# Block-sparse attention with a channel mixer: near outputs and part of the second dense unit turned by VectorE and transfers instead of TensorE

## The chip, the core and the metric

The program runs on one core of a Trainium2 chip. The metric is the device time of one execution in microseconds (us). The engines are PE (TensorE, with PEld for its weight loads), DVE (VectorE), ACT (ScalarE), POOL (GpSimd) and SP (SyncE, which here only issues DMA transfers). Each engine runs its instructions strictly in program order and waits on semaphores for the others.

## What is computed

The reference is block-sparse attention of 4 batches, 8 heads, 768 tokens and 64 channels, in blocks of 32 tokens, and behind it a channel mixer on the 512 joined channels.

```python
mask = abs(blk_i - blk_j) <= 1           # neighbours
mask |= first and last block, as rows and as columns
mask[qb, sampled_blocks[qb]] = True      # 3 sampled blocks each
attn = softmax(where(mask, q @ k.T / 8, -1e9)); x = attn @ v   # (4, 768, 512)
xk = mu_k * x + (1 - mu_k) * x_prev      # x_prev: one token earlier
xr = mu_r * x + (1 - mu_r) * x_prev
out = sigmoid(xr @ w_r) * (relu(xk @ w_k) ** 2 @ w_v)
```

All of it is float32; the mixer's products are made as three products of rounded halves each.

## The kernel before

**Units.** Batches go in two pairs. For each pair there is first a dense unit (`wide_pair`): the 64 rows of the first and last block, against all 768 keys, in four steps hp of two heads (names `sw`, `pw`, `tw`, `ptw`, `o_-1`). Then come eleven near units m = 0 to 10 (`near_unit`): two blocks of each of two batches, 128 rows, against eight key blocks (names `s`, `p`, `tb`, `o`). In the order of all 24 units the first dense unit is number 0, the second number 12; the near units are 1 to 11 and 13 to 23.

**Steps of a unit.** PE makes scores, DVE scales, masks and takes the minimum (L439), ACT makes exponentials and their sums (L444), PE multiplies the probabilities by V (L565 for near, L603 for dense units). For that product the probabilities must lie with keys on partitions. For units up to 7 PE turns them (`turn`, L453) and ACT or DVE copies them out of PSUM. For near units from number 8 (`CARRY`) DVE turns 32x32 blocks (`carry`, L471) and four transfers, each from 32 partitions to 128, put the blocks in place. The dense units use PE: 12 transposes for each hp, in three groups of four.

**Outputs.** `finish` divides by the sums on DVE (`x`, L628), PE turns x in four transposes (`tx`, L622), and ACT copies the result into the mixer's input `xt` (L658). The kernel also holds a path (`apart`) that turns x on DVE and lays it by transfers; with OUT = 30 no unit takes it.

**Mixer.** Each of 6 tiles of 128 tokens for each pair has gates (`r`, L752), hidden layers (`h`, L772, L784) and products (`v`, L798). The last four tiles run as two double tiles (the hidden layer of both in one matmul). `split_x` makes the rounded halves of a tile's input from `xt` on DVE, ACT and POOL.

**Order.** Every step is numbered in the order of the program text; `ORDER` is a table of these numbers, written out, that sets the order on every engine. `PICK` is a table of letters that sets the engine of each copy, rounding and difference. SP's transfers stand in that order too: weights, Q, K (`KR`) and V (`VR`) for the units, probabilities (`p`), and outputs. V of a near unit fills all four `VR` buffers in turn, so V of the next unit loads only when PE has used them. Buffers named `pt` (4 of them) hold x, turned probabilities and, in the double tiles, gates.

Of the kernel before, what the change touches and what calls it, by code (L numbers as in the profile page):

```python
# [159 lines left out]
def block_sparse_attention_channel_mix(ctx: ExitStack, tc: tile.TileContext, kt, kd, kw, qw, qn, vt, vn, vw, blocks, own_near, mu_k, mu_r, w_k, w_v, w_r, out):  # L160
# [187 lines left out]
    def load_wide(pr, i):  # L348
# [5 lines left out]
        def pair(hp):  # L354
            keys, values = ([], [])
            for i in range(PAIR):
# [8 lines left out]
                plan.add(SP, lambda r=r, hp=hp, i=i: nc.sync.dma_start(r.ap, kw[pr, hp, :, i]), writes=[(r.owner, *{k: 0 for one in r.keys for k in one})], size=wire(393216, 3072))  # L365
# [10 lines left out]
    def load_near(pr, m, i):  # L376
# [17 lines left out]
        for j in range(PAIR):  # L394
# [175 lines left out]
    def wide_pair(b, hp, q, t0, both, values, o, L):  # L570
# [15 lines left out]
        for row in range(2):  # L586
            keys = [(row, 0), (2 + row, W)]
            exp(ps_[row], slice(0, S), keys, nm, 2 + row, L, 2 * hp + row, t0 + W_EXP)
            parts += [(ps_[row], keys, lambda x, n=n: x[:, n * P:(n + 1) * P]) for n in range(6)]
            if b in CARRY_WIDE:  # L590
                carry(ps_[row], keys, f'w{b}_{hp}_{row}', 6)
        pts = [] if b in CARRY_WIDE else [turn(parts[4 * i:4 * i + 4], f'w{b}_{hp}_{i}') for i in range(3)]
        for row in range(2):
# [3 lines left out]
            def pv(h=h, mine=mine):  # L597
                for n, i in enumerate(mine):
                    for r in range(0 if pts else QB):
                        at = r * S // QB + n * BLK  # L600
                        nc.tensor.matmul(o.ap[ROWS[r], h * D:(h + 1) * D], ps_[h % 2].ap[:, at:at + BLK], values[r // PAIR].ap[:, n * P + h % 2 * D:n * P + (h % 2 + 1) * D], start=n == 0, stop=n == 5, skip_group_check=True)
                    for one, V in zip(HALF, values if pts else ()):
                        nc.tensor.matmul(o.ap[one, h * D:(h + 1) * D], pts[i // 4].ap[:, i % 4, one], V.ap[:, n * P + h % 2 * D:n * P + (h % 2 + 1) * D], start=n == 0, stop=n == 5, skip_group_check=True)  # L603
            plan.add(PE, pv, reads=([(pts[i // 4],) for i in mine[::2]] if pts else [(ps_[row], (row, 0), (2 + row, W))]) + [(V.owner, *V.keys) for V in values], writes=[(o, (hp, row))])

    def finish(b, m, i, o, parts, L):
# [19 lines left out]
        def divide():  # L626
            if apart or not DEAL:
                nc.vector.tensor_tensor(out=x.ap.rearrange('p (h d) -> p h d', d=D), in0=o.ap.rearrange('p (h d) -> p h d', d=D), in1=R.ap.unsqueeze(2).to_broadcast([P, H, D]), op=ALU.mult)  # L628
                return
            for half in range(2):  # L630
                nc.vector.tensor_tensor(out=x.ap.rearrange('p (c f k) -> p c k f', c=CC, k=QB)[:, :, 2 * half:2 * half + 2], in0=o.ap.rearrange('p (c k f) -> p c k f', c=CC, k=QB)[:, :, 2 * half:2 * half + 2], in1=R.ap.rearrange('p (c h) -> p h c', h=2)[:, half].unsqueeze(2).unsqueeze(3).to_broadcast([P, CC, 2, BLK]), op=ALU.mult)
# [440 lines left out]
```

## Time and profile before

| | |
|---|---|
| median of 3 runs | 528.49 us (528.47 to 529.82) |
| the profiled execution | 528.91 us, span 527.1 us |
| granted TensorE clock, mean | 0.997 |
| PE busy | 510.8 us, 97% |
| DVE / ACT / POOL busy | 355.7 / 313.2 / 213.5 us |
| DMA | 103.23 MB, 48164 packets, mean 196 GB/s |

The span is the time from the first to the last instruction; the execution is 1.8 us longer. The busy time of PE counts each matmul to its modelled end, so that a step in PE's stream is better read from the start of one group to the start of the next. The share of DMA is the mean busy share of the core's 16 DMA engines.

### The profile page before, as it was taken

The numbers are of one execution on the slowest core, as the hardware profiler recorded it, in microseconds if no ns is written. First come the engines' busy times: TensorE is split into PE (matmuls) and PEld (weight loads), VectorE is DVE, ScalarE is ACT, GpSimd is POOL, SyncE is SP. The second block draws the span as 40 slices with busy tenths as digits, with TensorE's granted clock in tenths as the row PEclk, the third lists the DMA queues.
The fourth block names the chain that finished last, engine by engine and source line by source line (L and its number), as shares of the span: only waits on it lengthen the run. The fifth ranks groups of instructions, "written<-read, shape, count | busy, mean of one in ns | idle before, by whom it ended". The sixth has DMA issues, their size and how long they took to land.

```text
span 527.1 us, 17633 instructions
## 1 busy us (share of the span) xinstructions
PE 510.8 (97%) x6935; PEld 407.3 (77%) x6935; DVE 355.7 (67%) x866; ACT 313.2 (59%) x785; POOL 213.5 (41%) x257
## 2 busy tenths in 40 slices
PE   7897999999999999999999999999999999999997
PEld 2464688779877887787987888888877788888886
DVE  4799899885887766566757676774898475441502
ACT  2789899876835574656565576467574365414430
POOL 0542545424611622552083174643261246605540
PEclk8999999999999999999999999999999999999999
DMA  8999794563678797468667787877866314010002
GB/s 289 405 321 353 277 351 146 174 222 101 183 244 240 231 319 239 170 224 248 209 191 237 244 259 215 234 238 203 238 198 184 113 31 141 0 67 15 1 0 80
DMA packets 48164, 103.23 MB, mean 196 GB/s; under 512 B 6929, under 2 KB 23442, under 8 KB 48082
## 3 DMA queue, kind: packets, MB, share of 16 engines
q1 hardware_dynamic: 47794, 101.72, 60.6%
q8 instruction: 54, 0.88, 0.7%
q10 hardware_dynamic: 288, 0.39, 0.2%
q14 instruction: 28, 0.23, 0.1%
HBM read 80.07 MB, written 6.29 MB: 164 GB/s over the span
## 4 chain that ended last, share of the span: by engine, by line
PE 77%; DMA 7%; SPq 5%; DVE 4%; ACT 4%; issue 2%; ACTq 0%; DVEq 0%
PE v L798 21%; PE o L565 7%; PE s L535 5%; PE r_0p L752 5%; PE r_1p L752 5%; PE h_3p L772 4%; PE h_2p L772 4%; PE h_1p L772 3%; PE h_0p L772 3%; DMA VR<-vn 2%; SPq L418 2%; DMA VR<-vt 2%; SPq L475 2%; PE sw L581 2%; DMA p<-tb 2%
## 5 line engine op out<-in xcount | busy, mean ns | idle before, releaser
L798 PE MATMUL v<-w,k 128*128 128x512 f32 (+1 forms) x600 | 141.5, 388 | 0.1
L798 PEld LDWEIGHTS v<-w,k 128*128 128x128 f32 x600 | 107.8, 188 | 25.0 <-issue 1.2
L439 DVE CUSTOM_DVE_ANT_1 p<-s,near_mask 128x256 f32<-128x256 f32 x152 | 84.0, 628 | 23.5 <-DMA p<-tb 12.9
L444 ACT ACTIVATE p<-p,nm 128x256 f32<-128x256 f32 x152 | 76.2, 503 | 33.1 <-DVE nm L439 30.9
L471 DVE STREAM_TRANSPOSE tb<-p 128x1024 f32<-128x1024 f32 x30 | 37.2, 1242 | 16.9 <-ACT p L444 11.3
L535 PE MATMUL s<-KR,q 64*32 64x256 f32 x1216 | 38.4, 380 | 0.0
L182 POOL COPY KR<-keys 128x256 f32 (+2 forms) x54 | 22.9, 462 | 27.8 <-DMA keys<-kw 13.7
L801 DVE SCALAR_TENSOR_TENSOR z<-v,z 128x512 f32<-128x512 f32 (+1 forms) x25 | 16.3, 660 | 25.8 <-PE v L798 25.8
L565 PEld LDWEIGHTS o<-VR,p 128*32 128x32 f32 x1920 | 27.9, 110 | 6.7 <-issue 4.0
L565 PE MATMUL o<-VR,p 128*32 128x64 f32 x1920 | 30.8, 220 | 1.6 <-DMA VR<-vn 0.8
L752 PE MATMUL r_1p<-w,xr 128*128 128x512 f32 x120 | 31.3, 404 | 0.0
L752 PE MATMUL r_0p<-w,xr 128*128 128x512 f32 x120 | 30.6, 401 | 0.2 <-DVE z L801 0.2
L535 PEld LDWEIGHTS s<-KR,q 64*32 64x32 f32 x1216 | 20.9, 106 | 10.7 <-issue 2.1
L731 POOL TENSOR_TENSOR xr<-xr_1f,xr 128x256 fp32r<-128x256 f32 x10 | 7.4, 739 | 53.0 <-ACT xr L180 39.9
L444 ACT ACTIVATION_READ_ACCUMULATOR p<-p,nm 128x1 f32 x152 | 28.8, 189 | 0.0
L752 PEld LDWEIGHTS r_0p<-w,xr 128*128 128x128 f32 x120 | 21.9, 188 | 6.5 <-PE sw L581 0.6
L762 POOL TENSOR_TENSOR h_0k<-h_0k 128x512 f32<-128x512 f32 x10 | 10.6, 1063 | 38.7 <-ACT k L761 38.7
L752 PEld LDWEIGHTS r_1p<-w,xr 128*128 128x128 f32 x120 | 21.6, 188 | 5.4 <-ACT h_3k L760 0.4
L772 PE MATMUL h_2p<-xk,w 128*128 128x256 f32 x192 | 25.1, 285 | 0.0
L772 PE MATMUL h_3p<-xk,w 128*128 128x256 f32 x192 | 25.1, 286 | 0.0
L772 PE MATMUL h_0p<-xk,w 128*128 128x256 f32 x192 | 25.0, 284 | 0.0
L772 PEld LDWEIGHTS h_1p<-xk,w 128*128 128x128 f32 x192 | 23.5, 189 | 1.6 <-ACT h_0k L760 0.8
(226 smaller groups left out, 1086.7 us busy)
## 6 DMA issues: line engine op xcount, KB each, us to landing
VR<-vn SPq DMA_DIRECT2D x42, 512.0 KB, 4.6
VR<-vt SPq DMA_DIRECT2D x130, 128.0 KB, 3.3
p<-tb SPq DMA_DIRECT2D x120, 128.0 KB, 3.2
KR<-kd SPq DMA_DIRECT2D x18, 512.0 KB, 4.6
out<-z SPq DMA_DIRECT2D x23, 256.0 KB, 2.7
q<-qn SPq DMA_DIRECT2D x22, 256.0 KB, 4.5
keys<-kw SPq DMA_DIRECT2D x14, 384.0 KB, 5.5
raw<-w_k SPq DMA_DIRECT2D x4, 1024.0 KB, 7.4
```

Of the source, the lines that this page charges most:

```text
L182: engine(on).tensor_copy(to, of)
L418: nc.sync.dma_start(to[:, i], vt[bass.ds(sampled_block(nc.sync, pr, m, j * NRAND + i) + pr * NB, 1)].rearrange('o k b x -> (o k) (b x)'))
L439: nc.vector.tensor_tensor_reduce(out=dealt(p.ap[:, cs]), in0=cut(view()), in1=by, scale=-SCALE, scalar=3e+38 if first is None else nm.ap[: ...
L444: plan.add(ACT, lambda: nc.scalar.activation(p.ap[:, cs], p.ap[:, cs], AF.Exp, bias=nm.ap[:, col:col + 1], scale=-1.0, accum_out=L.ap[:, h ...
L471: plan.add(DVE, lambda: nc.vector.transpose(out=turned.ap.rearrange('p (k y c) -> p k y c', k=QB, c=BLK), in_=p.ap.rearrange('p (y k c) -> ...
L535: nc.tensor.matmul(s.ap[ROWS[j], row, a * 256:(a + 1) * 256].rearrange('p (x g a) -> p g a x' if carried else 'p (x a g) -> p g a x', g=2, ...
L565: nc.tensor.matmul(o.ap[ROWS[j], h * D:(h + 1) * D], held[gi][1](i, g, j), VR[values[j % PAIR][g]].ap[:, j // PAIR, h * D:(h + 1) * D], st ...
L752: nc.tensor.matmul(pr.ap[:, 0:512], xr.ap[:, a, c, :], wr[c].ap[:, w, :], start=c == 0 and m == 0, stop=c == CC - 1 and m == 2)
L762: plan.add(POOL, lambda: nc.gpsimd.tensor_tensor(out=kk.ap, in0=kk.ap, in1=kk.ap, op=ALU.mult), reads=[(kk,)], writes=[(kk,)])
L772: nc.tensor.matmul(ph.ap[:, ff * PAIR * TT:(ff + 1) * PAIR * TT], wk[f // 4 * CC + c].ap[:, w, f % 4 * P:(f % 4 + 1) * P], xk.ap[:, a, c, ...
L798: nc.tensor.matmul(pv.ap[:, 0:width], hid[f][2](a), wv[f].ap[:, w, cs], start=f == 0 and m == 0, stop=f == FC - 1 and m == 2)
L801: plan.add(DVE, lambda pv=pv, cs=cs: nc.vector.scalar_tensor_tensor(out=z.ap[:, cs], in0=pv.ap[:, 0:width], scalar=unit, in1=z.ap[:, cs], ...
```

## The change

1. OUT goes from 30 to 9, so the outputs of near units from number 9 take the path `apart`: units 9 to 11 (m = 8 to 10 of the first pair) and 13 to 23 (all of the second), 14 by this count; the instructions show 14 too. x is turned by one DVE instruction whose read steps by four elements, and four transfers of 32x512 values lay it into `xt`, in pieces of 32 values (128 bytes).
2. The variant `DEAL`, off before, is removed.
3. CARRY_WIDE = (1,), AWAY = 4: in the second dense unit four of the six 128-key chunks of each head are turned by DVE and carried by four transfers of 64 KB (`carry_most`); the other two still by PE, one group of four for each hp instead of three. The product takes 32-row matmuls for the carried chunks and 64-row ones for the rest.
4. Keys of a dense unit come in one transfer of 768 KB for each hp instead of two of 384 KB (but for the first hp of the first unit).
5. SENT is empty, so its new branch does nothing.
6. ORDER and PICK are new: fewer ACT and more DVE copies of sampled keys among others.

```diff
-                plan.add(SP, lambda r=r, hp=hp, i=i: nc.sync.dma_start(r.ap, kw[pr, hp, :, i]), ...)
+                if i == PAIR - 1:
+                    plan.add(SP, lambda hp=hp: nc.sync.dma_start(whole[pr].ap[:, hp], kw[pr, hp]), ...)
...
+    def carry_most(p, keys, most, name):
+        size = QB * AWAY * BLK
+        turned = buf([P, size], F32, 'pt', PT_BUFS, f'tw{name}')
+        plan.add(DVE, lambda: nc.vector.transpose(out=turned.ap.rearrange('p (k y c) -> p k y c', k=QB, c=BLK), in_=p.ap[:, 0:size].rearrange('p (y k c) -> p k y c', k=QB, c=BLK)), reads=[(p, *keys)], writes=[(turned,)])
+
+        def away():
+            for r in (0, 2, 1, 3):
+                nc.sync.dma_start(p.ap[:, r * AWAY * BLK:(r + 1) * AWAY * BLK], turned.ap[r * BLK:(r + 1) * BLK])
+        plan.add(SP, away, reads=[(turned,)], writes=[(p, most)], ...)
...
-                carry(ps_[row], keys, f'w{b}_{hp}_{row}', 6)
-        pts = [] if b in CARRY_WIDE else [turn(parts[4 * i:4 * i + 4], f'w{b}_{hp}_{i}') for i in range(3)]
+                carry_most(ps_[row], keys, (row, 'most'), f'w{b}_{hp}_{row}')
+        away = AWAY if b in CARRY_WIDE else 0
+        rest = [x for i, x in enumerate(parts) if i % 6 >= away]
+        pts = [turn(rest[i:i + 4], f'w{b}_{hp}_{i // 4}') for i in range(0, len(rest), 4)]
...
-            plan.add(DVE, lambda: nc.vector.transpose(out=flip.ap.rearrange('p (k c f) -> p k c f', k=QB, f=BLK), in_=x.ap.rearrange('p (c k f) -> p k c f', k=QB, f=BLK)), ...)
+            plan.add(DVE, lambda: nc.vector.transpose(out=flip.ap.rearrange('p (k c f) -> p k c f', k=QB, f=BLK), in_=x.ap.rearrange('p (c f k) -> p k c f', k=QB, f=BLK)), ...)
...
-CARRY_WIDE = ()
-OUT = 30
-DEAL = OUT <= NP * NM
+SENT = ()
+CARRY_WIDE = (1,)
+AWAY = 4
+OUT = 9
...
-    "turn": "AAAADDAAAAADAAAAAADDAAAAAADDAAAAAADADDAAAAADDAADDDDA",
+    "turn": "AAAAAAAADAADDAAADAAAAADAAAAADDADDAAADDDDAADAA",
...
-    2, 13, 0, 119, 3, 15, 14, 24, 20, 22, 28, 27, 23, 45, 44, 21, 64, 65, 84, 25, 31, 85, 112, 16, 29, 114, 30, 33,
+    22, 3, 4, 14, 20, 0, 1, 116, 16, 24, 44, 28, 23, 2, 13, 30, 29, 21, 25, 31, 47, 33, 32, 50, 35, 34, 36, 37, 49,
```

On PE, in the second pair, behind the scores of its unit 2 and among the hidden layers of tile 4 (`h_4`), before and now:

```order
L535 MATMUL s_2_0_4770<-KR,q_2_4244 32x8x32 x16
L535 MATMUL s_2_1_4790<-KR,q_2_4244 32x8x32 x16
L622 MATMUL tx_0_4808<-ident,x_0_4757 128x128 x4
L772 MATMUL h_4_3p<-xk_4_4162,w_938 128x256 x6
L772 MATMUL h_4_3p<-xk_4_4162,w_1433 128x256 x6
```

```order
L789 MATMUL h_4_1p<-xk_4_4309,w_794 128x256 x6
L553 MATMUL s_2_1_4807<-KR,q_2_4557 32x8x32 x16
L553 MATMUL s_2_0_4830<-KR,q_2_4557 32x8x32 x16
L789 MATMUL h_4_2p<-xk_4_4309,w_901 128x256 x6
L789 MATMUL h_4_2p<-xk_4_4309,w_1404 128x256 x6
```

The four transposes of x of unit 0 (`tx_0`) are gone from the row; score and hidden matmuls follow each other.

On DVE, in the same pair, around the division of unit 0 (`x_0`), before and now:

```order
L439 ISA p_1_1_4502,nm_1_1_4503<-s_1_1_4445,near_mask 128x32x8
L439 ISA nm_1_1_4503 128x1
L471 STREAM_TRANSPOSE tb_1_1_4723<-p_1_1_4502 128x1024
L624 RECIPROCAL R_0_4615<-R_0_4615 128x8
L628 TENSOR_TENSOR x_0_4757<-o_0_4522,R_0_4615 128x512
L618 TENSOR_SCALAR R_1_4759<-L_1_4443 128x8
```

```order
L447 ISA nm_1_0_4686 128x1
L645 RECIPROCAL R_0_4472<-R_0_4472 128x8
L648 TENSOR_TENSOR x_0_4756<-o_0_4617,R_0_4472 128x512
L479 STREAM_TRANSPOSE tb_1_0_4765<-p_1_0_4685 128x1024
L652 STREAM_TRANSPOSE xf_0_4767<-x_0_4756 128x512
L743 SCALAR_TENSOR_TENSOR xr_4_1f_4798<-xr_4_1d_4785,mk,xt_4_3489 128x128
```

Behind the division now stands the turn of x into `xf_0`, one transpose of probabilities (`tb_1_0`) later.

On SP, in the second dense unit, where keys and V of that unit are loaded, before and now:

```order
L475 DMA p_10_0_3503<-tb_10_0_3704 128x1x256 x4
L365 DMA keys_3184<-kw 128x768 x2
L369 DMA VR_68<-vw 128x768
L369 DMA VR_71<-vw 128x768
L369 DMA VR_69<-vw 128x768
L369 DMA VR_70<-vw 128x768
L369 DMA VR_68<-vw 128x768
L369 DMA VR_69<-vw 128x768
L393 DMA KR<-kd 128x1024
L802 DMA out<-z_2_1_3443 128x512
L369 DMA VR_70<-vw 128x768
L369 DMA VR_71<-vw 128x768
```

```order
L493 DMA pw_0_1_3747<-tww_0_1_3769 128x1x128 x4
L370 DMA VR_68<-vw 128x768
L370 DMA VR_69<-vw 128x768
L493 DMA pw_0_0_3764<-tww_0_0_3794 128x1x128 x4
L370 DMA VR_71<-vw 128x768
L661 DMA xt_5_720<-xf_10_3897 128x4x32 x4
L370 DMA VR_70<-vw 128x768
L493 DMA pw_1_1_3871<-tww_1_1_3907 128x1x128 x4
L493 DMA pw_1_0_3951<-tww_1_0_4031 128x1x128 x4
L370 DMA VR_68<-vw 128x768
```

The carried probabilities (`pw` from `tww`) and the laid output of unit 10 (`xt` from `xf_10`) now stand between the loads of V; the keys have gone ahead of this place.

## Rows read from the trace of the kernel before

**Rows 1.** The page's part 1: busy us, share of the span, instructions.
```profile
PE 510.8 (97%) x6935; PEld 407.3 (77%) x6935; DVE 355.7 (67%) x866; ACT 313.2 (59%) x785; POOL 213.5 (41%) x257
```

**Rows 2.** Busy us (instructions) of PE, PEld, DVE, ACT, POOL by stretch; clock; DMA.
```profile
0.00:85.00 85.00, 74.71 (x1225) 47.77 (x1225) 70.95 (x153) 66.71 (x163) 34.76 (x49) 0.98 0.91 326
180.00:255.00 75.00, 74.93 (x1101) 59.97 (x1100) 49.01 (x142) 43.34 (x103) 26.72 (x38) 1.00 0.74 235
255.00:450.00 195.00, 193.43 (x2727) 161.20 (x2725) 134.32 (x328) 114.75 (x308) 90.23 (x109) 1.00 0.66 195
450.00:527.10 77.10, 73.70 (x341) 60.47 (x339) 24.38 (x49) 23.36 (x44) 28.08 (x30) 1.00 0.07 28
```

**Rows 3.** Timeline of PE: start, us, line, operation; first and last moved output.
```profile
182.80 0.66 PE L622 MATMUL tx<-ident,x 128*128 128x128 f32 x4
183.21 1.17 PE L798 MATMUL v<-w,k 128*128 128x512 f32 x4
...
449.13 0.60 PE L622 MATMUL tx<-ident,x 128*128 128x128 f32 x4
449.48 2.82 PE L798 MATMUL v<-w,k 128*128 128x512 f32 x11
```

**Rows 4.** Timeline of all engines behind the last near unit's product.
```profile
445.72 1.99 PE L565 MATMUL o<-VR,p 128*32 128x64 f32 x128
447.78 0.69 DVE L628 TENSOR_TENSOR x<-o,R 128x512 f32<-128x512 f32 x1 [5.49 <-PE o L565]
450.98 0.59 ACT L658 COPY xt<-tx 128x512 f32<-128x512 f32 x1
460.51 0.77 DVE L731 TENSOR_TENSOR later<-xk_5f,later 128x512 fp32r<-128x512 f32 x1
466.97 2.96 PE L784 MATMUL h_3p<-later,w 128*128 128x512 f32 x12
```

**Rows 5.** Groups by line on DVE: count, busy us, mean ns, idle before.
```profile
L471 DVE STREAM_TRANSPOSE tb<-p 128x1024 f32<-128x1024 f32 x30 | 37.2, 1242 | 16.9 <-ACT p L444 11.3 <-ACT KR L180 3.2 <-DMA p<-tb 1.6
L439 DVE CUSTOM_DVE_ANT_1 p<-s,near_mask 128x256 f32<-128x256 f32 x152 | 84.0, 628 | 23.5 <-DMA p<-tb 12.9 <-PE s L535 10.3
L439 DVE CUSTOM_DVE_ANT_1 pw<-sw,wide_mask,nmw 128x384 f32<-128x384 f32 x16 | 9.6, 617 | 3.8 <-PE sw L581 3.1
```

**Rows 6.** SP's issues and landing of carried probabilities: ns and us, min/median/max.
```profile
L475 SPq DMA_DIRECT2D p<-tb x120: 542/596/1661, 139.5 to 437.1; - x120
DMA to landing us min/median/max: 2.5/3.2/5.2
```

**Rows 7.** Timeline of PE, second dense unit: some of its turns and products.
```profile
218.36 0.60 PE L453 MATMUL tw<-ident,pw 128*128 128x128 f32 x4
218.88 1.62 PE L603 MATMUL o_-1_3970<-VR,ptw 128*64 128x64 f32 x48
220.44 1.09 PE L453 MATMUL tw<-ident,pw 128*128 128x128 f32 x8
221.46 1.52 PE L581 MATMUL sw<-keys,qw 64*64 64x384 f32 x16
...
236.65 0.60 PE L453 MATMUL tw<-ident,pw 128*128 128x128 f32 x4
237.00 3.73 PE L798 MATMUL v<-w,k 128*128 128x512 f32 x15
```

**Rows 8.** Timeline of PE: a near unit's product and what follows.
```profile
270.42 1.99 PE L565 MATMUL o<-VR,p 128*32 128x64 f32 x128
272.34 1.67 PE L752 MATMUL r_1p<-w,xr 128*128 128x512 f32 x6
```

**Rows 9.** Transfers in 430 to 438 us, carried probabilities almost alone: packets, DMA share.
```profile
DMA packets 884, 0.82 MB, mean 103 GB/s; under 512 B 94, under 2 KB 883, under 8 KB 883
q1 hardware_dynamic: 883, 0.81, 44.8%
```

**Rows 10.** The same in 469 to 478 us: four outputs alone, 2 KB pieces.
```profile
DMA packets 576, 1.05 MB, mean 117 GB/s; under 512 B 64, under 2 KB 64, under 8 KB 576
q1 hardware_dynamic: 576, 1.05, 30.4%
```

**Rows 11.** ACT's exponentials of the dense units: count, busy us, mean ns.
```profile
L444 ACT ACTIVATE pw<-pw,nmw 128x768 f32<-128x768 f32 x16 | 14.9, 933 | 9.9 <-DVE nmw L439 9.2 <-ACT xr L180 0.7
```

**Rows 12.** Timeline of PE at the start: second scores, waiting for keys.
```profile
8.59 1.56 PE L581 MATMUL sw<-keys,qw 64*64 64x384 f32 x8 [1.63 <-DMA keys<-kw]
```

**Rows 13.** What SP waited for in 255 to 450 us: total, times, longest.
```profile
SPq L411 <- PE o L565: 11.9, 5, 3.6
SPq L418 <- PE o L565: 9.8, 3, 4.1
```

More of the change, by code (lines that the diff above doesn't have):

```diff
@@ L364, in pair @@
                     continue
-                plan.add(SP, lambda r=r, hp=hp, i=i: nc.sync.dma_start(r.ap, kw[pr, hp, :, i]), writes=[(r.owner, *{k: 0 for one in r.keys for k in one})], size=wire(393216, 3072))
+                if i == PAIR - 1:
+                    plan.add(SP, lambda hp=hp: nc.sync.dma_start(whole[pr].ap[:, hp], kw[pr, hp]), writes=[(whole[pr], *[(hp, b, h) for b in range(PAIR) for h in range(2)])], size=wire(786432, 6144))
             for i in range(PAIR):
@@ L393, in load_near, with send @@
             plan.add(SP, lambda: nc.sync.dma_start(K.ap[:, WINDOW:WINDOW + 4].rearrange('p n a x -> p (n a x)'), kd[pr, :, n - 1:n + 3].rearrange('p n x -> p (n x)')), writes=[(K, 'near')], size=wire(524288, 4096))
-        for j in range(PAIR):
+        for j in range(PAIR if i in SENT else 0):
+            def send(j=j):
+                for r in range(NRAND):
+                    at = sampled_block(nc.sync, pr, m, j * NRAND + r) + pr * NB
+                    nc.sync.dma_start(K.ap[:, (NRAND + 1) * j + r].rearrange('p a x -> p (a x)'), kt[bass.ds(at, 1)].rearrange('o p x -> (o p) x'))
+            plan.add(SP, send, reads=[(packed,)], writes=[(K, ('far', j))], size=wire(131072, 1024) * NRAND, parts=NRAND)
+        for j in range(0 if i in SENT else PAIR):
             def fetch(j=j, key=PAIR * i + j):
@@ L476, in carry @@
         plan.add(SP, away, reads=[(turned,), (p, *keys)], writes=[(p, *keys)], size=QB * wire(22500 * wide, 128 * wide), parts=QB)
+    def carry_most(p, keys, most, name):
[5 more added lines that the diff above has]
+                nc.sync.dma_start(p.ap[:, r * AWAY * BLK:(r + 1) * AWAY * BLK], turned.ap[r * BLK:(r + 1) * BLK])
+        plan.add(SP, away, reads=[(turned,)], writes=[(p, most)], size=QB * wire(22500 * AWAY, 128 * AWAY), parts=QB)
     def first_scores(pr, m, gi, s, q, keys):
@@ L598, in pv @@
                 for n, i in enumerate(mine):
[L599 to L600 removed]
+                    i -= away * (i // 6 + 1)
+                    for r in range(QB if n < away else 0):
+                        at = (r * away + n) * BLK
                         nc.tensor.matmul(o.ap[ROWS[r], h * D:(h + 1) * D], ps_[h % 2].ap[:, at:at + BLK], values[r // PAIR].ap[:, n * P + h % 2 * D:n * P + (h % 2 + 1) * D], start=n == 0, stop=n == 5, skip_group_check=True)
[L602 removed]
+                    for one, V in zip(HALF, values if n >= away else ()):
                         nc.tensor.matmul(o.ap[one, h * D:(h + 1) * D], pts[i // 4].ap[:, i % 4, one], V.ap[:, n * P + h % 2 * D:n * P + (h % 2 + 1) * D], start=n == 0, stop=n == 5, skip_group_check=True)
[L604 removed]
+            plan.add(PE, pv, reads=([(pts[0],), (ps_[row], (row, 'most'))] if away else [(pts[i // 4],) for i in mine[::2]]) + [(V.owner, *V.keys) for V in values], writes=[(o, (hp, row))])
     def finish(b, m, i, o, parts, L):
@@ L626, in divide @@
         def divide():
[L627 to L631, printed above, removed]
+            nc.vector.tensor_tensor(out=x.ap.rearrange('p (h d) -> p h d', d=D), in0=o.ap.rearrange('p (h d) -> p h d', d=D), in1=R.ap.unsqueeze(2).to_broadcast([P, H, D]), op=ALU.mult)
         plan.add(DVE, divide, reads=[(o, *parts), (R,)], writes=[(x,)])
```

31 lines of the change are left out of this document (13 added, 18 removed), and 208 rows, old and new, of the table ORDER.

## The prediction

> **What bounds the kernel now.** First the busy shares of the page: PE is busy for 97% of the span, no other engine for more than 67% [rows 1]. Then the stretches: from 180 to 450 us PE is idle for 0.07 and 1.57 us (75.00 less 74.93, 195.00 less 193.43) and its clock is 1.00, the upper of its two levels [rows 2]. So here the end is set by how much PE has to do: work taken from its stream moves everything behind it, as long as what PE waits for still comes in time. The first 85 us are another matter: PE is idle for 10.3 us, DMA is busy at 0.91 and DVE for 71 of 85 us [rows 2]; there the loads set the pace. Behind 450 us transfers hardly matter (0.07). The second thing to read is what is close to being full in the stretches where the change puts its new work: DMA stands at 0.74 from 180 to 255 us (the second dense unit and units 8 to 10) and at 0.66 from 255 to 450 us (near units of the second pair) [rows 2]. DVE has 49 of 75 and 134 of 195 us there.
>
> **Outputs turned elsewhere.** A group of four `tx` costs PE the time from its start to the start of the next group: 0.41 us for the first moved unit, 0.35 us for the last [rows 3]; the 14 moved groups lie between 0.35 and 0.56 and sum to 5.6 us. All 14 stand in PE's full stretches, so I count 5.6 us as gain. No wait of PE is added in their place, since the consumer is the mixer tile, far behind: by the new order, with durations from the rows, 20.9 us of PE work lie between the last near unit's product and the first hidden layer of the last double tile. Before, that product starts at 445.72 and the last rounded half of the tile is ready at 461.28, 5.7 us before PE comes to it at 466.97 [rows 4]. The old way from divided x (448.47) to `xt` (451.57) takes 3.1 us [rows 4]; the new one is a turn, four issues and a landing: 0.62 us (half of 1242 ns, [rows 5]) to 0.95 us, 4 x 0.6 and 3.2 us [rows 6], or 6.2 to 6.6 us. The tile is later by 3.1 to 3.5 us, so at least 2.2 of the 5.7 us of margin stay. Cost on PE: 0.
>
> **The stepped read.** No row shows a DVE turn with a stepped read. Below stands half of the 1024-value turn, 0.62 us; above, the same times 1.5, the ratio per value of the near softmax pass with its stepped write (628 ns for 256) to the dense one (617 ns for 384) [rows 5], so 0.95 us. Fourteen of them are 9 to 13 us of DVE time, 8 turns of carried probabilities 5 us, and PICK moves 15 key copies to DVE. ACT loses the `xt` copies. DVE at 0.65 to 0.69 of the two stretches has room for it: 0 on the path.
>
> **Second dense unit.** PE's 12 groups of `tw` here cost 0.35 to 0.53 us each (0.52 for one, 1.02 for two together, 0.35 for the last, [rows 7]), 5.4 us in all or 0.45 each; 8 go: 3.6 us. The product of one hp took 1.56 us (218.88 to 220.44) for 48 matmuls of 64 rows, 32 ns each [rows 7]; a near product takes 1.92 us for 128 matmuls of 32 rows, 15 ns each [rows 8]. Now there are 256 of the small kind (3.8 us) and 64 of the large (2.1 us), 5.9 us instead of 6.2: a gain of 0.3 us. If the change of shape cost something at each switch it would be a few tenths; I leave it. PE's gain in sum: 5.6 + 3.6 + 0.3 = **9.5 us**.
>
> **What it gives back: transfers.** From 180 to 255 us DMA is busy for 0.74 x 75 = 55.5 us. To it come 32 transfers of carried probabilities (64 KB in pieces of 512 bytes) and 12 of laid outputs (64 KB in pieces of 128 bytes), while PE's stretch shrinks to 75 - 1.1 - 3.6 - 0.3 = 70 us. The nearest row is the carried near probabilities, also from 32 partitions to 128, in pieces of 1 KB: 0.448 x 8 us x 16 engines / 883 packets = 65 ns a piece, or 0.82 MB in 3.6 busy us = 229 GB/s [rows 9]. A 64 KB transfer then costs 0.29 us if bytes count; if pieces count, 0.52 us with 512 bytes and 2.08 us with 128 bytes. For the carried ones I take the middle, 0.40 us x 32 = 12.8 us. For the laid ones I take bytes, 0.29 x 12 = 3.4 us: outputs of 2 KB pieces run at 1.05 MB in 2.7 busy us, 384 GB/s [rows 10], with all 128 partitions as source, so the row's lower rate can come from its 32 source partitions, which the laid ones share, as well as from its pieces; both ends stay for the range. Sum 55.5 + 12.8 + 3.4 = 71.7 against 70: 1.7 us too much. On the Trainium skill's page "DMA: Bandwidth & Descriptors", section "Why small descriptors are slow (HBM only)", transfers within SBUF keep 78% of the link's rate with 128-byte packets; by that a laid transfer would be 0.37 us and the sum 1.0 us more. No row here shows such a piece.
>
> Besides, the new path from scores to product in that unit is long: four softmax passes of 0.62 us [rows 5], two exponentials of 0.93 us with their sums, 2.2 us [rows 11], a turn of 0.62, 8 issues of 0.6 us and a landing of 3.2 us [rows 6], 13.3 us. By the new order 12.9 us of PE work lie between scores and product of the last hp and 13.8 us for the first, where two loads of V also stand in SP's row (0.8 us). Late by 0.4 and 0.3 us on medians, and by 2 us more where a landing takes 5.2 us; I put 1.8 us. Given back in all: 3.5 us. In the stretch from 255 to 450 us the 44 laid transfers by bytes are 13 us on 129 of then 190 us: hidden.
>
> **The start.** Merged keys save issues but put 768 KB ahead of the second half of the first keys, for which PE waits now [rows 12]; at the 326 GB/s of that stretch [rows 2] that is 2.4 us later, and the next scores need no further wait. I take 0 and keep 2 us either way.
>
> **Sum.** 528.9 (the profiled execution) - 9.5 + 3.5 = 522.9; that execution lies 0.4 us above the median of the runs, so **522.5 us**.
>
> **Rivals.** (a) Transfers fit and PE never waits: the full 9.5 us, 519.0 us. For it: PE is full today with DMA at 0.74, and loads can be asked for earlier. Against: V of the dense unit can't load before PE has freed its buffers. (b) SP's row: each laid output is four issues, 2.4 us [rows 6], that wait for a turn on DVE and stand ahead of the next unit's V. Their cover is the time in which SP waits for PE to free those buffers anyway, 21.7 us in 255 to 450 us [rows 13]; 11 units need 26.4 us. The 4.7 us without cover go to PE through late V: 527.2 us, and 528 with a late turn or two. This counts as no change. (c) Slower: pieces of 128 bytes cost by the piece. The stretch of the second dense unit then fills with transfers that PE waits for. With 1.8 us for the chains it decides where 55.5 + 12.8 + 12 x = 70 + 7.7, x = 0.78 us, or 24 ns a piece. At 40 ns a laid transfer is 1.28 us, transfers are 83.7 us, and the time is 522.5 + (13.7 - 1.7) = 534.5 us. At 65 ns the second stretch overflows too (129 + 92 against 190 us) and it would be 574 us. For it: the 1 KB pieces run at 229 GB/s where 2 KB ones run at 384 [rows 9, 10]. Against: 65 ns is for eight times the bytes. The Trainium skill, same page, section "Specifications", speaks for (c): 512 bytes is the least piece at line rate, and below it the engine reads, changes and writes back. It gives no time, and no run here shows one.
>
> **How the numbers follow.** Forecast 0.42, (a) 0.20, (b) 0.15, (c) 0.23. A measurement of this kernel tells 0.3%, 1.6 us, from no change: faster means under 526.9 us. Faster 0.62, same 0.15, slower 0.23. The range reaches down to (a) with 2 us from the start and a little of today's waits, 516.5, and up to (c) at 40 ns, 534.5; what lies outside is about 2 in 10, most of it above.
>
> **What would show it.** PE's busy time down by some 9 to 13 us; 40 instead of 96 `tx` and no wait behind the last tile's hidden layers; DMA share from 180 to 255 us at 0.9 or more, with waits of PE for `pw` or `VR` of 2 to 4 us in that unit; laid transfers that land within 3 to 4 us. If DMA stays near 0.8 there, (a) holds; if laid transfers take over 0.8 us of all engines each, (c). Wrong altogether would be a PE wait at the tiles' first gates in the second pair, or a first 85 us that moved by over 2 us.

## The result, and the profile after

The changed kernel takes 536.4 us in the median (532.19 to 539.12) against 529.15 us (528.47 to 530.30) of the kernel before in the same session: **1.013 times** the time, interval 1.0097 to 1.0163. It is slower, above the range that was given (516.5 to 534.5). Its profiled execution is the longest of its four: 539.12 us, span 537.4 us, mean clock 0.990. That is 10.3 us of span more than the trace of before; the medians differ by 7.2 us.

The page's part 1 of the changed kernel, and the stretches of [rows 2] in its trace (busy us of PE, PEld, DVE, ACT, POOL; clock; DMA share; GB/s):

```profile
PE 508.1 (95%) x6971; PEld 402.5 (75%) x6975; DVE 361.4 (67%) x882; ACT 304.0 (57%) x761; POOL 222.3 (41%) x266
```

```profile
0.00:85.00 85.00, 71.43 (x1195) 46.87 (x1200) 68.36 (x148) 65.03 (x156) 39.60 (x48) 0.96 0.90 318
180.00:255.00 75.00, 68.38 (x1019) 51.41 (x1027) 50.22 (x130) 36.37 (x84) 26.94 (x37) 1.00 0.79 229
255.00:450.00 195.00, 190.50 (x2736) 157.28 (x2721) 138.18 (x353) 111.92 (x298) 82.10 (x104) 0.99 0.77 222
450.00:537.40 87.40, 83.45 (x503) 68.49 (x501) 31.30 (x66) 24.64 (x45) 32.56 (x34) 1.00 0.10 31
```

PE did lose work, but it now stands idle for 6.6 us from 180 to 255 us where it was full before, and for 4.5 us from 255 to 450. DMA isn't near full in either stretch (0.79 and 0.77). The longest waits of PE in the whole trace (us in total, times, longest) are all for transfers, yet small:

```profile
PE o L583 <- DMA VR<-vt: 2.5, 2, 2.1
PE sw L599 <- DMA keys<-kw: 2.4, 1, 2.4
PE o L583 <- DMA VR<-vn: 2.2, 1, 2.2
```

Waits alone don't show where the time went, because the new order also moves mixer work on PE from one place to another. So I counted PE's own work: the number of matmuls of each form that stand ahead of a given product in PE's row, times the duration of that form at full clock. It is an estimate, good to 1 or 2 us in a row of the table, and it takes no price for a change between forms. All of it is 502.1 us before and 494.0 us after, 8.1 us less. The time at which a product starts, less the work ahead of it, is how late PE is there:

| near unit's product (number in the order) | start, before / after | late, before / after / v_one_after (below) |
|---|---|---|
| 4 | 84.42 / 87.44 | 21.5 / 24.2 / 21.0 |
| 9 | 172.77 / 174.77 | 24.9 / 26.9 / 26.6 |
| 11, ahead of the second dense unit | 207.32 / 211.24 | 24.9 / 31.6 / 29.9 |
| 13, behind it | 252.65 / 262.11 | 25.2 / 38.5 / 37.8 |
| 23, the last | 445.72 / 451.86 | 24.3 / 42.7 / 35.5 |
| end | 527.1 / 537.4 | 25.0 / 43.4 / 36.1 |

The lateness grows by 18.4 us: 2.0 up to number 9, 4.7 up to 11, 6.6 across the second dense unit, 5.1 in the second pair. 18.4 less 8.1 is the 10.3 us of span. The last tiles add nothing. The first 85 us cost this trace 2.7 us (number 4); v_one_after, which has the same order there, shows nothing of it. The granted clock of that stretch was 0.96 here and 1.00 in v_one_after, so in this trace it may well be the clock. This is also the longest of the four executions, 2.7 us above their median.

What stands in the places where it grows is SP's row of issues. The timeline of SP in the changed kernel through the second dense unit (start, us, line, transfer, count; the time of a row includes waits inside it):

```profile
209.04 2.75 SPq L661 DMA_DIRECT2D xt<-xf  x4
211.89 0.57 SPq L819 DMA_DIRECT2D out<-z  x1
212.51 0.43 SPq L394 DMA_DIRECT2D KR<-kd  x1
213.03 3.58 SPq L493 DMA_DIRECT2D pw<-tww  x4
216.71 1.03 SPq L370 DMA_DIRECT2D VR<-vw  x2
217.83 2.51 SPq L493 DMA_DIRECT2D pw<-tww  x4
220.44 0.54 SPq L370 DMA_DIRECT2D VR<-vw  x1
221.08 2.66 SPq L661 DMA_DIRECT2D xt<-xf  x4
223.78 1.39 SPq L370 DMA_DIRECT2D VR<-vw  x1
225.27 5.71 SPq L493 DMA_DIRECT2D pw<-tww  x8
231.08 1.82 SPq L370 DMA_DIRECT2D VR<-vw  x1
233.00 2.48 SPq L493 DMA_DIRECT2D pw<-tww  x4
```

Each row starts within 0.1 us of the end of the one before. In the trace of before SP stood still between such rows, for 2.3 and 6.9 us in these:

```profile
221.90 0.38 SPq L802 DMA_DIRECT2D out<-z  x1
224.55 0.81 SPq L369 DMA_DIRECT2D VR<-vw  x2
225.41 0.42 SPq L378 DMA_DIRECT2D q<-qn  x1
232.69 0.33 SPq L393 DMA_DIRECT2D KR<-kd  x1
```

From 180 to 415 us SP has five gaps of over 0.8 us between its rows in the changed kernel, 7.3 us in all, and none from 206.8 to 297.5; in the trace of before there are 15 in the same stretch, 50.2 us in all. The records of the issues sum to 186.4 us of those 235, where they summed to 134.9. V of a dense or near unit (`VR`) stands in that row, and it can be asked for only once PE has used the buffer. **Theory S:** the issues themselves fill SP's row, V and carried probabilities come late, and PE stops. **Theory D**, the first one: the loss is the second dense unit's carried probabilities alone.

### The profile page after: what moved, and what is told of

Read it like the earlier page. It is cut to its first block, busy times and chain, and to the rows that moved or that the text cites. A ratio compares the mean times of both kernels' runs of the same rounds, so it can differ in the third digit from the quotient of the medians.

```text
span 537.4 us, 17890 instructions
## 1 busy us (share of the span) xinstructions
PE 508.1 (95%) x6971; PEld 402.5 (75%) x6975; DVE 361.4 (67%) x882; ACT 304.0 (57%) x761; POOL 222.3 (41%) x266
## 3 DMA queue, kind: packets, MB, share of 16 engines
q1 hardware_dynamic: 80962, 107.49, 64.9%
## 4 chain that ended last, share of the span: by engine, by line
PE 61%; DMA 15%; SPq 11%; DVE 4%; issue 4%; ACT 3%; POOL 1%; DVEq 0%; POOLq 0%; ACTq 0%
PE v L815 19%; PE o L583 6%; DMA p<-tb 4%; PE s L553 4%; DMA VR<-vn 3%; PE r_0p L769 3%; PE r_1p L769 3%; DMA raw<-w_k 3%; SPq L483 3%; PE h_2p L789 3%; PE h_3p L789 3%; PE h_1p L789 2%; PE h_0p L789 2%; SPq L661 2%; SPq L493 2%
## 5 line engine op out<-in xcount | busy, mean ns | idle before, releaser
L583 PEld LDWEIGHTS o<-VR,p 128*32 128x32 f32 x1920 | 29.4, 112 | 11.3 <-issue 6.4
L583 PE MATMUL o<-VR,p 128*32 128x64 f32 x1920 | 32.6, 223 | 5.2 <-DMA VR<-vt 2.5
L452 ACT ACTIVATE pw<-pw,nmw 128x768 f32<-128x768 f32 x16 | 15.0, 936 | 22.2 <-DVE nmw L447 20.3
L789 PEld LDWEIGHTS h_2p<-xk,w 128*128 128x128 f32 x192 | 24.2, 194 | 1.5 <-issue 0.6
L789 PEld LDWEIGHTS h_3p<-xk,w 128*128 128x128 f32 x192 | 23.5, 188 | 2.3 <-issue 1.8
```

Of the source, the lines that this page charges most:

```text
L452: plan.add(ACT, lambda: nc.scalar.activation(p.ap[:, cs], p.ap[:, cs], AF.Exp, bias=nm.ap[:, col:col + 1], scale=-1.0, accum_out=L.ap[:, h ...
L583: nc.tensor.matmul(o.ap[ROWS[j], h * D:(h + 1) * D], held[gi][1](i, g, j), VR[values[j % PAIR][g]].ap[:, j // PAIR, h * D:(h + 1) * D], st ...
L789: nc.tensor.matmul(ph.ap[:, ff * PAIR * TT:(ff + 1) * PAIR * TT], wk[f // 4 * CC + c].ap[:, w, f % 4 * P:(f % 4 + 1) * P], xk.ap[:, a, c, ...
```

## The experiments

Ratios are to the kernel before in the same session, with their 95% interval.

**The changed kernel once more**, with no edit, as the measure for the runs beside it:

> The changed kernel once more, for a second profile and for the times that the next three are set against. Its four runs gave 532.2 to 539.1 us, the profiled one being the slowest. If the waits of the first trace belong to the kernel, the same places show them again: PE waits in the second dense unit for the carried probabilities and for V (5.6 us between 200 and 262 us in the first trace) and a first 85 us with 13 us of idle PE. If they belong to one slow execution, this run is near 532 us and PE's idle time is some 7 us less. I expect 534 to 538 us, with the first kind.

538.64 us, 1.0183 (1.0121 to 1.0246), just above what was expected. In its trace PE is idle for 13.2 us in the first 85 us and for 6.9 us from 180 to 255, so these belong to the kernel.

**One part of the change undone: u_dense, u_out, u_both.** The dense unit's probabilities by PE again, or the outputs by PE and ACT again, or both, at the numbers that the new order gives to the DVE turn and the transfers:

```diff
-                carry_most(ps_[row], keys, (row, 'most'), f'w{b}_{hp}_{row}')
+                mosts.append(turn(parts[6 * row:6 * row + 4], f'w{b}_{hp}_most{row}', ...))
...
-        if apart:
+        if False:
             flip = buf(...)            # u_out: PE tr and ACT copies instead
```

> The changed kernel with the second dense unit's probabilities turned by PE alone again (12 transposes for each hp, 64-row products); all else and the order are kept, save that an operation which finds no free buffer stands back until there is one. Theory 1, the loss is in the second dense unit: its carried probabilities cost more than the 3.6 us they take from PE, since the product in two shapes takes 11.2 us where it took 6.2 and SP issues without a pause there; undone, the time is 529 to 532 us. Theory 2, the laid outputs are the loss (56 issues on SP, 28672 pieces): then PE gets 3.9 us more to do and nothing back, 538 to 541 us. Theory 3, the new order and PICK are the loss: about the same, 536 us.

> The changed kernel with the outputs of units from number 9 turned by PE and copied by ACT again; all else and the order are kept, save that an operation which finds no free buffer stands back, and PE's turn stands at least one other PE step behind its unit's product. Theory 1 (second dense unit): PE gets 5.6 us back and SP loses 56 issues of 0.64 us, so waits of near units for V and probabilities (some 4 us behind 262 us) and of the dense unit go; 535 to 539 us. Theory 2 (laid outputs): 528 to 531 us. Theory 3 (order): 540 us or more.

> Both undone: no laid outputs, no carried probabilities in the second dense unit; what stays of the change is the new order and PICK and the merged transfers of keys. Theories 1 and 2: near the kernel before, 528 to 532 us, the start being 2 us longer in the new order. Theory 3: 535 us or more. If it is under 527 us, order and merged keys are a gain by themselves, and the two moves lose all of it and more.

Measured: 1.0398 (1.0334 to 1.0463), 1.1173 (1.1094 to 1.1252), 1.1488 (1.1383 to 1.1594). They tell nothing of the parts, though theory 3 left such times open for the last two: the steps put back block PE and ACT where they stand (in u_out PE's products `v` wait 5.4 us for ACT's `xt`, and for V 7.4 us). What follows is only that the table of the order and the moved steps belong together.

**The same with places chosen for the steps put back: u_dense2, u_out2, u_both2.** The PE turns go behind the next PE work, the copies ahead of their reader. In the last two some of ACT's copies came to stand behind readers of the same mixer tile, which then took older values.

> The changed kernel with the second dense unit's probabilities turned by PE alone, placed with care this time: the two more groups of transposes for each hp stand behind the third group's place on PE, and their copies stand just ahead of the next step of their engine that needs a later PE result (the first form put them where the transfers stood, and ACT and PE waited for each other). Theory 1 (dense unit): 5 to 8 us go against the changed kernel's 538.6, 530.5 to 533.5 us. Theory 2 (outputs): PE gets 3.9 us more, 540 to 543 us. Theory 3 (order): 537 to 540 us.

> The changed kernel with outputs of units from number 9 turned by PE two PE steps behind the product and copied by ACT just ahead of its next step that needs a later PE result. Theory 1: PE gets 5.6 us back, SP 36 us less to issue, waits of 3 to 5 us go: 537 to 541 us. Theory 2 (outputs are the loss): 529 to 533 us. Theory 3 (order): 541 to 545 us.

> Both undone with the same care: what stays of the change is order, PICK and merged keys. Theory 1: 529 to 534 us (2 us of it from the start). Theory 2: 529 to 534 us. Theory 3 (order): 537 us or more, since with PE's turns back the new order has no gain to set against its waits.

Measured: u_dense2 1.0201 (1.0121 to 1.0282), u_out2 1.0396 (1.0325 to 1.0468), u_both2 1.0572 (1.0493 to 1.0652). u_dense2, 541.0 us, is as slow as the changed kernel, so theory D falls in the form in which I stated it. In that unit SP then has time and waits for the product (the view of SP's waits in u_dense2):

```profile
SPq L431 <- PE o_-1_3980 L693: 13.7, 2, 9.6
```

With this order, and the steps put back in these places, the carried probabilities are worth nothing net that the runs could tell: what PE saves in turns is about what they cost. The other two, 551.6 and 559.6 us, remain bound to their order: u_out2 is slower than any of the three theories gave, and u_both2 lies in the range that theory 3 left open.

**One part alone in the kernel before: b_out.** Laid outputs for the same units, the turn at the place of PE's turn and the four transfers at the places of ACT's copies:

```diff
-OUT = 30
-DEAL = OUT <= NP * NM
+OUT = 9
```

> One part of the change alone, on the kernel before with its own order and PICK: outputs of units from number 9 are turned by DVE (stepped read) and laid by four transfers each, at the places of PE's turn and ACT's copies, nothing else is moved. PE has 14 groups less, 5.6 us. Theory 1 (the loss of the change is in the second dense unit, outputs are near what was forecast): SP gets 56 issues, 36 us, in rows that are 0.6 to 0.77 full there, and some V comes late, 2 to 4 us; 524 to 527 us against 528.4. Theory 2 (laid outputs are the loss): 530 us or more. Theory 3 (the new order is the loss): 523 to 525 us.

562.65 us, 1.0604 (1.0532 to 1.0676). From the waits of POOL and SP in b_out:

```profile
POOL xt L708 <- DMA xt<-xf: 45.4, 5, 13.2
SPq L705 <- DVE xf L696: 15.4, 2, 10.1
SPq L705 <- DVE nm L500: 14.1, 3, 10.5
```

SP stands in front of DVE's turn with V queued behind it, and POOL's one-column copy stands in front of the landing with keys and tiles queued behind. That is rival (b) in its plain form, and the new order avoids it: in the changed kernel SP's waits ahead of laid transfers are 3.7 us in all from 180 to 450 us. It doesn't show what the change costs with its own order.

**More issues, same bytes: lay_twice.** Each laid transfer cut in two, 112 issues instead of 56:

```diff
-    nc.sync.dma_start(xt[b, t].ap[:, k, :, at:at + BLK], flip.ap[(PAIR * k + j) * BLK:(PAIR * k + j + 1) * BLK])
+    for g in range(2):
+        nc.sync.dma_start(xt[b, t].ap[64 * g:64 * g + 64, k, :, at:at + BLK], flip.ap[... + 16 * g:... + 16 * g + 16])
```

> The changed kernel with each laid transfer cut in two (16 partitions to 64 instead of 32 to 128): 112 issues on SP instead of 56, the same bytes, the same pieces, the same order. Theory S: SP's row is what binds; in the trace of the changed kernel SP issues from 208 to 385 us with hardly a gap, at 0.64 us an issue, so 44 more issues in the near units of the second pair are 28 us of a row that has little room, and 12 more in the second dense unit's stretch 8 us: 552 to 570 us against 538. Rival P (bytes and pieces of transfers, or the place of waits in the order): nothing is added that counts, 536 to 541 us.

560.28 us, 1.0607 (1.054 to 1.0674), some 22 us more than the changed kernel for 56 more issues of 0.61 us (34 us of SP's row). As theory S expects. The lower clock, 0.985 against 0.990 over the trace, is some 2.5 us of it.

**The issues on another engine: lay_act**, and **b_act**, the same on the kernel before:

```diff
-    nc.sync.dma_start(xt[b, t]..., flip...)
+    nc.scalar.dma_start(xt[b, t]..., flip...)
```

> The changed kernel with the laid transfers issued by ACT instead of SP, each just ahead of ACT's next step that needs a later DVE result, so that ACT would wait there anyway; ACT is 57% busy and gets 34 us of issues. Theory S: SP has 36 us more room, V and probabilities come earlier, 4 to 8 us of PE's waits go: 529 to 534 us. Rival P: 536 to 541 us. If ACT's row now holds up exponentials, 541 us or more.

> The kernel before, its order and PICK, with outputs of units from number 9 turned by DVE and laid by transfers that ACT issues (where ACT's copies stood or later), and with the one-column copies on POOL put just ahead of their first reader. Only the issuing engine and the place of those copies differ from the run with laid outputs on SP, which took 562.7 us. Theory S: SP's row is as in the kernel before, PE has 5.6 us less to do: 524 to 528 us. Rival: the landing of laid outputs itself is too late for the mixer in this order, or ACT waits for DVE's turns: 535 us or more.

1.0321 (1.0243 to 1.0399) and 1.0653 (1.0599 to 1.0706). Slower, though SP is rid of 56 issues; two of the waits of SP in lay_act:

```profile
SPq L884 <- DMA xt<-xf: 11.8, 1, 11.8
SPq L483 <- DMA xt<-xf: 7.0, 3, 5.2
```

SP's issues now wait for the landing of ACT's transfers (31 us with two more such rows, of 6.8 and 5.6 us). No data asks for it: in that trace the transfers of SP and of ACT count on the same eight semaphores, and the waits are for one that a transfer of ACT was the last to use (at 270.5 us an issue waits for semaphore 104, on which it is to count itself). So it is the program's sharing of semaphores. Both runs miss the forecast of S and fall where their expectations put ACT's waits and late landings (541 and 535 us or more). SP does have gaps of over 0.8 us in lay_act again, 42.2 us from 180 to 415 us, some of them these waits; with ACT's row changed as well, the run neither bears S out nor refutes it. In b_act PE waits 12.9 us for carried near probabilities.

**A disputed term by itself: switches.** The dense product changes between 32-row and 64-row matmuls four times for each head instead of once:

```diff
-                for n, i in enumerate(mine):
+                for k, n in enumerate((0, 4, 1, 5, 2, 3) if away else range(6)):
```

> The changed kernel with the product of the second dense unit in another order of chunks, so that 32-row and 64-row matmuls take turns: 4 changes of shape inside each of the 8 products instead of 1, the same matmuls otherwise. In the trace of the changed kernel a product whose inputs are there takes 0.97 us, 0.74 by its matmuls at the pitches of the near and of the first dense unit. If the rest is paid at each change of shape, 0.11 us each, a product takes 1.30 us and the time is 2.6 us longer, 540 to 542 us. If it's a cost of the group and not of the change, 0.97 us stay and the time is 538.

537.68 us, 1.0135 (1.0077 to 1.0192): no different from the changed kernel. PE's timeline of two heads' product, in the changed kernel and then in switches, whose profiled execution was the longest of its four (542.96 us):

```profile
222.32 0.65 PE L622 MATMUL o_-1_3980<-VR,pw 128*32 128x64 f32 x32
222.91 0.45 PE L624 MATMUL o_-1_3980<-VR,ptw 128*64 128x64 f32 x8
223.29 0.65 PE L622 MATMUL o_-1_3980<-VR,pw 128*32 128x64 f32 x32
223.88 0.45 PE L624 MATMUL o_-1_3980<-VR,ptw 128*64 128x64 f32 x8
224.26 1.66 PE L769 MATMUL r_1p<-w,xr 128*128 128x512 f32 x6
```

```profile
226.79 0.32 PE L622 MATMUL o_-1_3980<-VR,pw 128*32 128x64 f32 x8
227.04 0.34 PE L624 MATMUL o_-1_3980<-VR,ptw 128*64 128x64 f32 x4
...
229.44 0.50 PE L769 MATMUL r_1p<-w,xr 128*128 128x512 f32 x1
```

Two heads take 1.94 us (222.32 to 224.26) with three changes between shapes and 2.65 us (226.79 to 229.44) with eight, so a change costs 0.14 us. The Trainium skill's page "TensorEngine Tiling (Array Packing)", section "Key Properties", says that a change of tiling mode drains the engine; the traces agree as far as each change costs time, here 0.14 us. The edit adds 0.71 us to each of four such pairs of heads, 2.8 us of PE work, at a clock of 1.00 in both traces (222 to 249 and 226 to 253 us). So the price is paid at each change, yet the time is not the 540 to 542 us that this was to give. That says little, since 2.8 us is no more than such an interval is wide. PE's waits for `pw` in this unit, 1.3 us in the changed kernel, are gone from the trace of switches, which fits added work that fills waits; it isn't shown.

**Fewer issues, same bytes: v_one_after and v_one_before.** From unit 9 on V of the three sampled blocks comes as one transfer of three fixed blocks instead of three transfers, at 28 places: 56 issues less, and no addresses for SP to read there. It is the opposite of lay_twice, and done to both kernels:

```diff
             def gather(w=w, j=j, more=more, unit_no=i):
+                if unit_no >= 9:
+                    nc.sync.dma_start(VR[w[0]].ap[0:NRAND * BLK]..., vt[pr * NB + 4:pr * NB + 4 + NRAND]...)
+                    return
```

> The changed kernel, but from unit 9 on V of the three sampled blocks comes as one transfer of three fixed neighbouring blocks (so the sampled blocks' values are not the asked ones): the same bytes and pieces, one issue instead of three in 28 places, and no address to read first. Nothing else is moved. Theory S (SP's row binds): SP loses 56 issues of 0.7 us, 39 us, just where the change added 56 laid and 32 carried ones; V lands earlier and most of the gain that was forecast comes back: 522 to 528 us. Rival P (the waits come from the new order, from landing times or from other engines' rows): 535 to 540 us.

> The same edit on the kernel before. Theory S: its SP row had 0.6 to 0.77 of its time in issues and PE waited for 1.6 us only behind 255 us, so next to nothing is to be had: 526.5 to 529 us. If it falls by more than 3 us, an SP row with gaps binds too, and the gain of the same edit on the changed kernel says less.

v_one_after 531.88 us, 1.0003 (0.9961 to 1.0045); v_one_before 529.84 us, 1.0012 (0.9978 to 1.0046). The first lies between the two forecasts, above the 522 to 528 of S and below the 535 to 540 of P: S holds for a part of the loss only. The same edit gives the changed kernel 7 to 10 us (7.3 us of span between the two traces; 1.0183 against 1.0003 is 9.5 us) and the kernel before nothing. SP's timeline in one unit, of the changed kernel and of v_one_after:

```profile
268.82 6.02 SPq L483 DMA_DIRECT2D p<-tb  x8
275.11 2.09 SPq L426 DMA_DIRECT2D VR<-vt  x3
277.30 2.75 SPq L661 DMA_DIRECT2D xt<-xf  x4
280.14 0.56 SPq L379 DMA_DIRECT2D q<-qn  x1
280.75 1.87 SPq L394 DMA_DIRECT2D KR<-kd  x1
282.72 0.38 SPq L419 DMA_DIRECT2D VR<-vn  x1
283.36 2.10 SPq L426 DMA_DIRECT2D VR<-vt  x3
```

```profile
275.03 0.58 SPq L426 DMA_DIRECT2D VR<-vt  x1
275.71 2.71 SPq L664 DMA_DIRECT2D xt<-xf  x4
278.51 0.57 SPq L379 DMA_DIRECT2D q<-qn  x1
279.13 0.43 SPq L394 DMA_DIRECT2D KR<-kd  x1
281.44 0.33 SPq L419 DMA_DIRECT2D VR<-vn  x1
281.81 0.43 SPq L426 DMA_DIRECT2D VR<-vt  x1
```

The second has a gap of 1.9 us ahead of 281.44, the first none. From 243 to 415 us SP has 16 gaps of over 0.8 us again, 34.0 us in all (three of 5.4 us in the changed kernel), and PE is full again in the second pair (stretch of v_one_after as in [rows 2]), though DMA is busier than in the changed kernel (0.82 against 0.77):

```profile
255.00:450.00 195.00, 193.96 (x2846) 160.07 (x2830) 144.43 (x361) 113.10 (x300) 87.02 (x110) 1.00 0.82 221
```

In the table above the lateness of v_one_after falls by 2.3 us in the second pair, where the changed kernel's grows by 4.2. This is the run that settles S for the second pair.

**Keys: keys_two.** The dense unit's keys in two transfers again:

```diff
-    nc.sync.dma_start(whole[pr].ap[:, hp], kw[pr, hp])
+    [nc.sync.dma_start(whole[pr].ap[:, hp, b], kw[pr, hp, :, b]) for b in range(PAIR)]
```

> The changed kernel with the keys of a dense unit in two transfers of 384 KB for each hp again, at the same place of the order. If the merged transfers are what makes the first 85 us longer (PE's first wait for keys is 2.4 us where it was 1.6, and PE is idle for 13.3 us where it was 10.5), 535 to 537 us. If it's the new order there, 538 us as before or, by 7 more issues on SP, 1 us more.

538.98 us, 1.0202 (1.0134 to 1.0271). As the changed kernel: these runs show neither a gain nor a loss from merged keys.

**The dose in the dense unit: carried_twice.** Each carried transfer of the second dense unit cut in two, 64 issues instead of 32:

```diff
-    nc.sync.dma_start(p.ap[:, r * AWAY * BLK:(r + 1) * AWAY * BLK], turned.ap[r * BLK:(r + 1) * BLK])
+    for g in range(2):
+        nc.sync.dma_start(p.ap[64 * g:64 * g + 64, ...], turned.ap[r * BLK + 16 * g:r * BLK + 16 * g + 16])
```

> The changed kernel with each carried transfer of the second dense unit cut in two (16 partitions to 64): 64 issues instead of 32, the same bytes and pieces. Theory S: SP issues without a gap from 208 to 246 us, so 32 more issues of 0.6 us, 19 us, are paid nearly in full there, less what later units make up: 546 to 558 us. Rival P: 536 to 541 us.

563.74 us, 1.0619 (1.0536 to 1.0702): about 25 us more than the changed kernel for 32 issues of 0.59 us, 19 us of SP's row, and above the 546 to 558 us of S. The largest wait of PE in carried_twice:

```profile
PE o_-1_3988 L623 <- DMA pw<-tww: 10.7, 9, 2.3
```

The clock is a large part of the 25 us: it was 0.90 from 180 to 255 us of that trace, and 0.967 over all of it against 0.990, which is up to 12 us of PE's 508. The rest, some 13 us, is less than the 19 us of issues. So SP's row has little slack in this unit, and PE's waits for `pw` grow from 1.3 to 10.7 us, but an added issue isn't paid in full by itself.

**Relief from an earlier unit on: v_all_after.** As v_one_after, from unit 5:

> As v_one_after, from unit 5 on instead of unit 9: V of the three sampled blocks is one transfer of three fixed neighbouring blocks (not the asked ones) in 36 places. v_one_after came to the time of the kernel before and lost its waits behind 255 us; what PE still waited for between 150 and 255 us was V of unit 8 (3.3 us, its loads still in three issues each), V of unit 10 (1.6) and sampled keys (2.5). Theory S for this stretch too: those go, 3 to 5 us less than v_one_after, 524 to 527.5 us. If the rest of the missing gain is PE's own (two shapes in one product, 1.5 us) and the start of the new order (2 us) alone, the time stays at 529 to 531 us.

531.52 us, 1.0032 (0.9994 to 1.007): no faster than v_one_after and above the 524 to 527.5 us of S, a miss. The loss ahead of the dense unit isn't in those issues.

**The issues on POOL: lay_pool.**

> The changed kernel with the laid transfers issued by POOL instead of SP, each just ahead of POOL's next step that needs a later DVE result. POOL is busy for 41% and idle for long stretches. If an issue costs POOL about what it costs SP (0.65 us), SP's row is freed by 36 us and POOL holds nobody up: 529 to 534 us, near the kernel before. If POOL's row holds up the roundings that PE waits for, as ACT's did (547.8), 540 us or more.

644.76 us, 1.2154 (1.2089 to 1.2218). One row of the queues (packets, MB, share) and one of POOL's waits in lay_pool:

```profile
q0 software_dynamic: 1792, 3.67, 2.8%
```

```profile
POOL xt L725 <- issue: 111.2, 40, 6.0
```

Issued by POOL the transfers go through another queue, and POOL stands for 111.2 us ahead of 40 of its 56 issues, 2.8 us each. The view names no releaser, but the times point to one: 43 of the 56 issues start 0.30 or 0.31 us after the transfer before them has landed, and no issue starts earlier than that. Its other work comes late by that.

## Why the prediction was wrong, step by step

**The bound.** That PE was full from 180 to 450 us was right, and work did leave it: 8.1 us by count, or 6.3 with the changes of shape below, where the sum said 9.5. Busy time fell by 2.7 us instead of 9 to 13: besides the dense product, which grew, the clock was lower (0.990 against 0.997 is 3.6 us of 508).

**The step that failed** is the part on what the change gives back: 3.5 us in the sum, where the lateness of PE grew by 18.4 us in the trace, 1.8 of it changes of shape. It weighed the new transfers by the busy share of the DMA engines and by landing times, and left SP's row to rival (b). Both sides of that were off:

- DMA was priced right in the sum, by luck. Its time is 60.6% of 527.1 us before and 64.9% of 537.4 us after (the row of q1), 319.4 and 348.8 us: 29.4 us more for 32 + 56 transfers; the prediction's prices give 12.8 + 16.2 = 29.0. By the size of the pieces in the trace, though, the carried transfers took 7.9 us of the 16 engines where 12.8 stood, and the laid ones 24.6 us where 16.2 stood. It predicted a stretch that overflows, and the measured share is 0.79; by the prediction's own sign that spoke for rival (a), 519.0 us, which the time refutes.
- The time of SP was not counted at all in the dense unit, and in rival (b) only for 11 units of the second pair, against waits summed over a whole stretch [rows 13]. Those 21.7 us of waits lie where they lie; an issue uses up a wait only if it stands in it. In the dense unit alone, 32 carried and 12 laid issues of 0.6 us are 27 us, in a stretch in which SP had gaps of 18.2 us before (five of those 15, 205 to 255 us). Rival (b) named the right mechanism and gave it 4.7 us and "no change"; what v_one_after takes back, with 56 issues less in its whole run, is 7 to 10, and the loss in and ahead of the dense unit comes on top.

**Terms that were mis-sized.** The dense product: eight heads at 0.97 us are 7.8 us against four of 1.56 us before, 6.2 [rows 7]; a loss of 1.5 us where 0.3 of gain stood, 1.8 us in all, because I left out the change of shape, 0.14 us each. The stepped turn of x took 1105 ns, above the upper bound of 0.95 us [rows 5]; the turn of dense probabilities 708 ns, where half of a longer one, 0.62 us, was taken. That neither cost time was argued (DVE is busy for 67%) and not tested. Lines of DVE in the changed kernel:

```profile
L652 DVE STREAM_TRANSPOSE xf<-x 128x512 f32<-128x512 f32 x14 | 15.5, 1105 | 2.1 <-DMA pw<-tww 2.0
L489 DVE STREAM_TRANSPOSE tww<-pw 128x512 f32<-128x512 f32 x8 | 5.7, 708 | 6.9 <-DMA pw<-tww 4.3 <-ACT z L773 2.5
```

**What held.** 40 transposes `tx` remain, no wait stands behind the last tile's hidden layers, and the merged keys show no effect (keys_two). The first 85 us moved by 2.7 us in the trace, more than the 2 us allowed, but not in v_one_after. Rival (c) did not come to pass: in the trace the 28,672 pieces of 128 bytes took 13.7 ns each in the mean, 0.44 us a laid transfer, below the 24 ns and 0.78 us from which it decides. They do cost more by the byte: pieces of 512 bytes took 30.8 ns and those of 1 KB 57.2 ns, so 128-byte pieces moved at about half the rate (9.3 against 17.9 GB/s an engine). The Trainium skill's statement that transfers between SBUFs don't pay for small packets (page "DMA: Bandwidth & Descriptors", section "Why small descriptors are slow (HBM only)", whose figure of 78% is for a remote transfer) doesn't agree with that. Laid transfers in the changed kernel (issue ns, then landing us, min/median/max):

```profile
L661 SPq DMA_DIRECT2D xt<-xf x56: 611/639/1615, 189.8 to 457.8; - x56
DMA to landing us min/median/max: 2.4/2.9/5.7
```

**What stays open.** v_one_after still ends 11.1 us later, measured against PE's own work, than the kernel before (36.1 against 25.0), which eats the 8.1 us saved. Some 1.8 of it are the changes of shape; nearly all the rest arises by number 13, in and just ahead of the dense unit. There SP's row has no gap in v_one_after either (none over 0.8 us from 180 to 243 us), and carried_twice shows that it has little slack. But with the row relieved by u_dense2 the unit was no faster, and SP waited for PE instead, so SP's row is shown as a bound there only for more issues, not for fewer, and the cause of the 11.3 us by which PE of the changed kernel falls behind from number 9 to number 13 stays open but for the changes of shape. The 4.7 us from number 9 to 11 were not separated; v_all_after didn't take them away. What the laid outputs alone cost could not be read from u_out2 or b_out, each bound to its order. Whether another order keeps the 8.1 us was not tried. No version here beats the kernel before.

## What to carry to other kernels

Count a queue's issues as work of the engine that issues them, unit by unit: number of transfers times the issue time, against the period of the unit, and only then look at bandwidth. Spare time of such a queue that a wait view sums over a stretch is not a store from which new issues can draw; what counts is whether the issues stand ahead of a load that can't be asked for earlier. A cheap test is to cut or merge some transfers at equal bytes in both kernels, as lay_twice and v_one did here: if only one of the two kernels answers, its row of issues is a likely bound. Read the clock of each trace with it, since in carried_twice up to half of the loss was clock.

## What was not expected of the hardware

- These issues cost 0.6 us of SP each, whether they move 64 KB of short pieces or half of it (0.639 and 0.608 us in the medians of the changed kernel and lay_twice), so cutting a transfer nearly doubles its price there.
- A change between 32-row and 64-row matmuls takes PE 0.14 us.
- Moving issues from SP to ACT made SP wait for the landing of ACT's transfers, 31 us in lay_act, through semaphores that both use in this program.
- An issue on POOL took 0.76 us, and none started before the transfer ahead of it had landed; 43 of 56 came 0.3 us behind that.
- Pieces of 128 bytes within SBUF took 13.7 ns each of a DMA engine, those of 1 KB 57.2 ns: eight times the bytes in four times the time.
- A turn of 32x32 blocks on DVE whose read steps by four elements took 1105 ns for 512 values in each partition, against 708 ns for as many values read in runs of 32.
